# Moving the two-operand steps of attention + gated MLP from GpSimd to VectorE, under a refitted order of issue

## The chip, the core and the metric

One core of a Trainium2 chip runs the whole program in one launch. The metric is the device time of that launch in microseconds; the program ahead of the change was timed in three runs, and one more execution was profiled. TensorE (PE, with its weight loads as PEld), VectorE (DVE), ScalarE (ACT), GpSimd (POOL) and SyncE (SP, which issues every DMA) run their own streams in order, and wait for each other by semaphores.

## What is computed

Eight batches of 12-head attention over 448 positions with head size 64 and a capped score, then a gated MLP with a spatial mix:

```python
B, H, S, D = 8, 12, 448, 64                      # float32 throughout
scores = cap * tanh((q @ k.T) / sqrt(D) / cap)   # cap = 30
attn = softmax(scores)                           # denominator + 1e-9
x = concat_heads(attn @ v)                       # (8, 448, 768)
h = relu(x @ w_in)                               # w_in 768 x 1024
u, v = h[..., :512], h[..., 512:]
v_n = (v - mean(v)) / sqrt(var(v) + 1e-6)
v_s = einsum('ts,bsd->btd', w_spatial, v_n) + b_spatial[:, None]
out = (u * v_s) @ w_out                          # w_out 512 x 768
```

## The kernel before

**Work.** Heads go in pairs: 48 pairs, six to a batch. For one pair PE makes the scores (`sc`, into `ps_s`, 28 tile products of 64x224), ACT takes tanh (L553) and exp (L558) into `tp`, and PE multiplies with `v` (`pv`, L568, into `ps_x`, which has one buffer). For the first eight pairs PE also sums the exponentials with a matrix of ones (`ones`, L610, read out by ACT at L614). DVE takes maxima (and from the ninth pair on the sums) over `tp` in trees (L588, L596, L598), which go to DRAM and back (`md`, `dt`); DVE finishes them there (L632, L637) and takes the reciprocal (L639). Two more DMAs carry it to DRAM (`rd`) and broadcast it back over the partitions (`rr`, L642). ACT meanwhile copies `ps_x` to `xf` (`xev`, L573).

**The two-operand steps.** Matrix products of the MLP are made from high and low parts in a rounded format, so each operand is split. For a pair: `xmul` multiplies `xf` by `rr` (L658), `xh` copies the high part into `xg` (L309), `xl` subtracts it for the low part (L305), `xt` copies a tail (L309). In the MLP of a batch (`moe`): four chains for v (L713 to L718) are read out, normalised on DVE (L736 to L744), copied to `vh` and subtracted to `vl` (L305); four chains for u (L691 to L693); four gate chains g over `vh`, `vl` (L782 to L787), each followed by `gmul` on DVE (L792, into `o`), a copy on ACT and `gl`, the subtraction into `xg` (L305); and six output chains (L807 to L809), evicted by ACT and stored. The first batch also splits the weights, on POOL, DVE and ACT (L374 to L381).

`BND_X`, `BND_G`, `BND_VN` name the engine of each step by a letter (P POOL, V DVE, A ACT): `"PAVA"` is xmul on POOL, xh on ACT, xl on DVE, xt on ACT; `"AP"` is a copy on ACT and a subtraction on POOL.

**What sets the order.** Nothing is ordered by hand. Each step is a task with an engine, a duration, dependences, buffers and a key; a key is the pair's number plus an offset from the table `BND_KEY` (or `BND_W_KEYS` for weights). `Plan.order` (L71) plays the tasks through a model of the engines: an engine that is free takes the task with the lowest key that is ready. In the model a PE task of another kind than the last one has `STICK` added to its key, and steps with the mark `lock` (all of POOL, most of DVE) never run together. A DMA lands by the formula at L155. The result is the order of issue; the chip's engines then follow it, each stream in order, waiting where data is late.

Of the kernel before, what the change touches and what calls it, by code (L numbers as in the profile page):

```python
# [21 lines left out]
QB = 14  # L22
# [20 lines left out]
class Plan:  # L43
# [27 lines left out]
    def order(self):  # L71
        free = dict(self.cap)
        turn = {}
        for t in sorted(self.tasks, key=lambda t: (t.key, t.seq)):
            for u in t.allocs:
                turn.setdefault(u.tag, []).append(u)
        turn = {g: (l[::-1]) for g, l in turn.items()}
        live = set()

        def lacks(t):  # L80

            need = {}
# [24 lines left out]
        while done < len(self.tasks):  # L107
            if not events:
                raise RuntimeError(f"no task can start: {[(t.name, t.key) for l in avail.values() for t in l][:20]} {free}")
            now = heapq.heappop(events)  # L110
            while events and events[0] <= now:
                heapq.heappop(events)
            while fins and fins[0][0] <= now:
                _, _, t = heapq.heappop(fins)
                done += 1
                for u in t.uses:
                    left[u] -= 1
                    if not left[u]:
# [12 lines left out]
            again = True  # L131
            while again:
                again = False
                for e in engs:
                    while pend[e] and pend[e][0][0] <= now:
                        avail[e].append(heapq.heappop(pend[e])[2])
                    if busy[e] > now or not avail[e]:
                        continue
                    fit = [t for t in avail[e] if not (t.lock and ports > now) and not lacks(t)]
                    if not fit:  # L140
                        continue
                    took = min(fit, key=lambda t: (t.key + (self.STICK if t.mode != mode and e == "T" else 0.0), t.seq))
                    avail[e].remove(took)
                    for u in took.allocs:
                        free[u.tag] -= 1
                        turn[u.tag].pop()
                        live.add(u)
                    took.start, took.end = now, now + took.dur
                    if e == "T":
                        took.end += self.TURN[took.mode] if took.mode != mode else 0.0  # L150
                        mode = took.mode
                    if took.lock:
                        ports = took.end
                    if e == "S":
                        dma = max(dma, took.end + 650.0) + took.lat  # L155
                        took.lat = dma + 1000.0 - took.end
                    busy[e] = took.end
                    out.append(took)
                    heapq.heappush(fins, (took.end + took.lat, took.seq, took))
                    heapq.heappush(events, took.end + took.lat)  # L160
                    heapq.heappush(events, took.end)
                    again = True
        self.length = now
        return out

MM, MMW, TR = 203, 229, 109
FF = 760
HW, HH, XL, XF = 475, 650, 50, 4 / 360  # L170
# [12 lines left out]
def dve(n):  # L183
    return 1.04 * n + 70
# [10 lines left out]
def gpc(n):  # L195
# [26 lines left out]
CAP_BITS = 0x42200000  # L222
ANY_KEY = dict(moe=0.5, span=12.0, mv=0.0)
ANY_W_KEYS = 2.0, 0.5, 8.0, 9.0, 1.0
BND_KEY = dict(ld=-21.99, vld=-20.83, sc=-4.54, th=26.01, ex=-43.74, pv=-2.08, sm=0.15,
               mx=0.17, dn=3.16, ev=8.76, x=0.83, moe=1.42, span=10.72, step=0.16, mv=-3.27)
BND_V_FIRST = 1
WARM, WARM_N = 9, 512
BND_W_KEYS = 13.02, 0.15, 11.56, 14.75, -2.19
PE_SUMS = 8  # L230
E_W = "PAV"
W_ORDER = (0, 1)
WO_N = 256
ANY_ENG = "P", "P", "P", "VP", "AAAA", "PVPV", "AP", "VP", "V"
BND_X, BND_G, BND_VN, BND_O = "PAVA", "AP", "AP", "A"


def attn_moe(ctx, tc, bounded, shared, qk, v, qk2, v2, cap, w_in, w_sp, w_out, out):
# [408 lines left out]
    def pair(b, hp):  # L647
# [22 lines left out]
        return prev  # L670

    def moe(b, xs):
        k0 = (b + 1) * H + KEY["moe"]
        step = KEY["span"] / 18.0
        xuse, xdep = [x for x, _ in xs], [d for _, d in xs]
        us, vs, gs = [], [], []
        ks = iter([k0 + n * step for n in range(18)])

        tags = iter(["s", "s", "acc", "acc"] * 5 if bounded and b == B - 1 else ["acc"] * 18)
        kv = lambda k: k + KEY["mv"]  # L680

        def u_part(js):
            for j in js:
# [206 lines left out]
```

## Time and profile before

| | |
|---|---|
| three runs, median | 772.05 us |
| lowest, highest | 768.41, 772.09 us |
| profiled execution | 772.54 us |
| its span (first to last instruction) | 770.7 us |
| PE busy | 738.4 us, 96% |
| DVE, ACT, POOL busy | 590.6, 498.2, 213.5 us |

The span is 1.8 us shorter than the execution's time. Busy time counts an engine as busy while any of its instructions is under way. The times of TensorE's clock come as "granted clock": 1.00 is 2.4 GHz, 0.50 is 1.2 GHz, and a value between is a mean of the two over a stretch. A "wait" is idle time of an engine, put down to the instruction that ended it.

### The profile page before, as it was taken

What the parts mean: (1) busy time and instruction counts of PE and PEld (TensorE: products, weight loads), DVE (VectorE), ACT (ScalarE), POOL (GpSimd) and SP (SyncE); (2) the same over time, 40 slices, a digit from 0 to 9 for tenths busy, and PEclk for the clock granted to TensorE, in tenths of its full rate; (3) what the DMA queues carried; (4) which work ended last, traced back from release to release, by engine and by line L of the source; (5) the groups of instructions that cost most, each with busy time, mean ns of one, the idle gap of its engine ahead of it and who ended that gap; (6) DMA issues with size and microseconds to landing.
All of it is one profiled execution on the core that took longest, in us unless ns stands there. A gap on an engine that the chain in (4) does not pass through costs nothing.

```text
span 770.7 us, 19011 instructions
## 1 busy us (share of the span) xinstructions
PE 738.4 (96%) x7865; PEld 599.8 (78%) x7865; DVE 590.6 (77%) x1062; ACT 498.2 (65%) x658; POOL 213.5 (28%) x177
## 2 busy tenths in 40 slices
PE   8888898989999999999899999999999999999997
PEld 5666587777788877877688877888788877888896
DVE  4898698979998878766996788966987788976230
ACT  7988765648773684766855598357865589356221
POOL 3233225341334114221043303331033203331230
PEclk9989899999999999999999999999999999999999
DMA  7546551324320540233422334025322335013002
GB/s 260 168 159 219 163 156 49 97 94 148 123 62 16 183 136 4 78 107 132 125 62 63 123 113 134 15 85 159 126 63 74 92 113 155 25 38 100 13 1 77
DMA packets 51141, 79.23 MB, mean 103 GB/s; under 512 B 22882, under 2 KB 35684, under 8 KB 51044
## 3 DMA queue, kind: packets, MB, share of 16 engines
q1 hardware_dynamic: 51044, 77.91, 32.2%
q8 instruction: 64, 1.05, 0.5%
q14 instruction: 33, 0.27, 0.1%
HBM read 66.04 MB, written 11.81 MB: 101 GB/s over the span
## 4 chain that ended last, share of the span: by engine, by line
PE 52%; DMA 15%; DVE 15%; ACT 5%; POOL 5%; issue 4%; SPq 2%; POOLq 0%; DVEq 0%; ACTq 0%
PE ps_s L546 8%; PE ps_x L568 8%; DVE red L588 7%; DMA dt<-md 4%; DMA rr<-rd 4%; PE ps_acc L807 4%; PE ps_acc L808 3%; PE ps_acc L691 3%; PE ps_acc L809 3%; DMA md<-st 3%; PE ps_acc L692 3%; PE ps_acc L693 3%; DMA rd<-dt 3%; PE ps_acc L716 2%; PE ps_acc L718 2%
## 5 line engine op out<-in xcount | busy, mean ns | idle before, releaser
L553 ACT ACTIVATE tp<-ps_s,capt 128x896 f32<-128x896 f32 x192 | 166.5, 909 | 33.1 <-PE ps_s L546 25.2
L588 DVE TENSOR_TENSOR red<-red,tp 128x896 f32<-128x896 f32 (+1 forms) x176 | 152.7, 882 | 13.1 <-ACT tp L558 12.8
L568 PE MATMUL ps_x<-tp,v 64*64 64x224 f32 x2688 | 148.2, 362 | 11.6 <-ACT xf L573 10.4
L558 ACT ACTIVATE tp<-tp,capt 128x1792 f32<-128x1792 f32 x96 | 154.2, 1606 | 2.2
L546 PE MATMUL ps_s<-raw 64*64 64x224 f32 x2688 | 148.9, 355 | 3.4 <-ACT tp L553 3.3
L658 POOL TENSOR_TENSOR xf<-xf,rr 128x448 f32<-128x448 f32 x48 | 69.1, 1440 | 289.0 <-DMA rr<-rd 271.5
L568 PEld LDWEIGHTS ps_x<-tp,v 64*64 64x64 f32 x2688 | 105.1, 138 | 41.6 <-ACT xf L573 12.7
L546 PEld LDWEIGHTS ps_s<-raw 64*64 64x64 f32 x2688 | 99.3, 134 | 40.8 <-issue 10.7
L588 DVE TENSOR_TENSOR red<-tp 128x896 f32<-128x896 f32 x88 | 96.9, 1122 | 27.8 <-ACT tp L558 27.8
L305 POOL TENSOR_TENSOR xg<-o,xg 128x448 fp32r<-128x448 f32 x32 | 50.2, 1573 | 79.4 <-ACT xg L309 79.3
L808 PE MATMUL ps_acc<-xg,wo_h 128*128 128x448 f32 x176 | 64.8, 368 | 5.5 <-POOL xg L305 5.5
L807 PE MATMUL ps_acc<-xg,wo_h 128*128 128x448 f32 x176 | 66.7, 379 | 0.9 <-DVE o L792 0.3
L691 PE MATMUL ps_acc<-xg,wi_h 128*128 128x448 f32 x174 | 63.8, 367 | 1.8 <-DVE stg L728 1.2
L809 PE MATMUL ps_acc<-xg,wo_l 128*128 128x448 f32 x176 | 64.2, 365 | 0.0
L692 PE MATMUL ps_acc<-xg,wi_h 128*128 128x448 f32 x174 | 63.2, 363 | 0.0
L693 PE MATMUL ps_acc<-xg,wi_l 128*128 128x448 f32 x174 | 63.0, 362 | 0.0
L632 DVE TENSOR_TENSOR dt<-dt 32x28 f32<-32x28 f32 x88 | 26.1, 318 | 47.9 <-DMA dt<-md 47.8
L573 ACT COPY xf<-ps_x 128x448 f32<-128x448 f32 x48 | 46.1, 959 | 19.0 <-DVE xg L305 15.5
L309 ACT COPY o<-ps_acc 128x448 f32<-128x448 f32 x44 | 23.4, 532 | 52.5 <-PE ps_acc L809 32.8
L596 DVE STREAM_TRANSPOSE red<-red 128x448 f32<-128x448 f32 x88 | 55.1, 632 | 0.6
L588 DVE TENSOR_TENSOR red<-red 128x448 f32<-128x448 f32 x88 | 54.7, 630 | 0.1
L716 PE MATMUL ps_acc<-wi_h,xg 128*128 128x512 f32 x132 | 54.0, 409 | 0.0
(116 smaller groups left out, 1241.7 us busy)
## 6 DMA issues: line engine op xcount, KB each, us to landing
raw<-in_qk SPq DMA_DIRECT2D x48, 448.0 KB, 3.7
v<-in_v SPq DMA_DIRECT2D x48, 448.0 KB, 4.1
rr<-rd SPq DMA_DIRECT2D x96, 112.0 KB, 3.0
out<-o SPq DMA_DIRECT2D x48, 224.0 KB, 2.1
w<-in_w_in SPq DMA_DIRECT2D x12, 512.0 KB, 6.0
xg<-in_w_out SPq DMA_DIRECT2D x12, 256.0 KB, 3.0
rd<-dt SPq DMA_DIRECT2D x48, 3.5 KB, 1.5
wy<-in_w_sp SPq DMA_DIRECT2D x3, 224.0 KB, 6.3
```

Source lines behind the costliest of these rows:

```text
L546: nc.tensor.matmul(ps.t[half_rows(h), e, c % 2 * QH:(c % 2 + 1) * QH], lhsT=raw.t[half_rows(e), S + c * D:S + (c + 1) * D], rhs=raw.t[half ...
L553: lambda o=g % 2 * PW, w=w, ps=ps, tp=tp: nc.scalar.activation(out=tp.t[:, o:o + 2 * w].rearrange("p (e q) -> p e q", e=2), in_=ps.t[:, :, ...
L558: lambda tp=tp, w=w: nc.scalar.activation(out=tp.t[:, :w], in_=tp.t[:, :w], func=AF.Exp, scale=ca), [ex], [tp],
L568: nc.tensor.matmul(x.t[half_rows(e), h, :QH], lhsT=vt.t[half_rows(h), (2 * c + e) * D:(2 * c + e + 1) * D], rhs=part(c, e)[half_rows(h)], ...
L588: tt = lambda o_, i0, i1, op=op: nc.vector.tensor_tensor(o_, i0, i1, op=op)
L691: nc.tensor.matmul(ps, lhsT=wi_h[:, c, fs], rhs=x[:, XH:], start=(c == 0), stop=False)
L692: nc.tensor.matmul(ps, lhsT=wi_h[:, c, fs], rhs=x[:, :S], start=False, stop=False)
L693: nc.tensor.matmul(ps, lhsT=wi_l[:, c, fs], rhs=x[:, XH:], start=False, stop=(c == NP - 1))
L716: nc.tensor.matmul(ps, lhsT=x[:, XH:][:, ts], rhs=wi_h[:, c, FH:], start=(c == 0), stop=False)
L807: nc.tensor.matmul(ps, lhsT=wo_h[:, c, ns], rhs=g[:, XH:], start=(c == 0), stop=False)
L808: nc.tensor.matmul(ps, lhsT=wo_h[:, c, ns], rhs=g[:, :S], start=False, stop=False)
L809: nc.tensor.matmul(ps, lhsT=wo_l[:, c, ns], rhs=g[:, XH:], start=False, stop=(c == 3))
```

## The change

Three two-operand steps go from POOL to DVE in all batches: `xmul` (48), `gl` (32) and `vl` (32). On POOL stay the scaling of weights, the low part of the spatial weights and the power of the normalisation. In the model, the landing of a DMA gets 300 ns more per transfer and a shorter tail for short ones, SP's issue cost and some PE costs are changed, and `STICK` is doubled. All offsets are new, and batch 0 adds offsets of its own, `KEY0`.

```diff
-    TURN, STICK = {"N": 200.0, "K": 150.0, "R": 190.0, "C": 145.0, "Q": 130.0}, 3.87
+    TURN, STICK = {"N": 200.0, "K": 150.0, "R": 190.0, "C": 145.0, "Q": 130.0}, 8.1
...
-                        dma = max(dma, took.end + 650.0) + took.lat
-                        took.lat = dma + 1000.0 - took.end
+                        dma = max(dma, took.end + 650.0) + took.lat + 300.0
+                        took.lat = dma + (1100.0 if took.lat > 1000.0 else 500.0) - took.end
...
-MM, MMW, TR = 203, 229, 109
+MM, MMW, TR = 202, 235, 109
-HW, HH, XL, XF = 475, 650, 50, 4 / 360
+HW, HH, XL, XF = 500, 550, 50, 4 / 400
...
-BND_KEY = dict(ld=-21.99, vld=-20.83, sc=-4.54, th=26.01, ex=-43.74, pv=-2.08, sm=0.15,
+BND_KEY = dict(ld=-9.15, vld=0.69, sc=-2.3, th=36.27, ex=-132.38, pv=-0.12, sm=8.79, mx=10.7, dn=-1.77, ev=-20.83, x=-6.67, moe=11.19, span=6.93, step=0.15, mv=-18.73)
+KEY0 = dict(ld=-49.29, vld=2.7, sc=-103.24, th=-27.84, ex=31.5, pv=-29.52, sm=-1.19, mx=-50.91, dn=-18.09, ev=-50.06, x=-27.36, moe=-7.29, mv=5.22)
...
-BND_X, BND_G, BND_VN, BND_O = "PAVA", "AP", "AP", "A"
+BND_X, BND_G, BND_VN, BND_O = "VAVA", "AV", "AV", "A"
+BND_X0 = "VAVA"
+E_SEV = "A"
...
-        kk = lambda name, n=0: at + KEY[name] + KEY["step"] * n
+        kk = lambda name, n=0: at + KEY[name] + KEY["step"] * n + (KEY0.get(name, 0.0) if b == 0 else 0.0)
```

The same sum of `KEY` and `KEY0` stands in `pair` and `moe`. `E_SEV` only gives the read-out of the ones sums a name for its engine, which stays ACT. Lines from L590 on in the changed file are two or three higher than in the old one (L553 becomes L555, L658 becomes L661).

**Place 1, ACT in the first batch, around the second pair's xh.** `tp<-ps_s` is a tanh, `tp<-tp` an exp, `xg<-xf` the copies xh (448 columns) and xt (64), `xf<-ps_x` is xev of a later pair, `wi_h` a weight's high part. Before:

```order
L558 ACTIVATE tp<-tp,capt 128x1792
L553 ACTIVATE tp<-ps_s,capt 128x448
L558 ACTIVATE tp<-tp,capt 128x1344
L309 CAST xg<-xf 128x448
L614 COPY sx<-ps_acc 128x7x32
L309 CAST xg<-xf 128x64
L309 CAST wi_h<-wy 128x512
L573 COPY xf<-ps_x 128x14x32
```

And now:

```order
L555 ACTIVATE tp<-ps_s,capt 128x896
L311 CAST xg<-xf 128x448
L555 ACTIVATE tp<-ps_s,capt 128x448
L311 CAST xg<-xf 128x64
L560 ACTIVATE tp<-tp,capt 128x1344
L575 COPY xf<-ps_x 128x14x32
```

The copy xh stands earlier against the tanh and exp of the next pairs, and still ahead of a later xev.

**Place 2, the low parts of the gate in the first batch.** They stand on POOL before (`vl` ends the v part, `xf<-xf,rr` is xmul, `xg<-o` is gl, `xg<-xg` a scaling of weights):

```order
L305 TENSOR_TENSOR vl<-stg,vl 64x512
L658 TENSOR_TENSOR xf<-xf,rr 128x448
L305 TENSOR_TENSOR xg<-o,xg 128x448
L374 TENSOR_SCALAR xg<-xg 128x256
L305 TENSOR_TENSOR xg<-o,xg 128x448
```

Now they stand on DVE, where `o<-ps_acc` is gmul, `red` the trees over `tp`, `xg<-xg` the splitting of `w_out`:

```order
L795 TENSOR_TENSOR o<-ps_acc,u 128x448
L590 TENSOR_TENSOR red_163<-red_163 128x448
L590 TENSOR_TENSOR red_162<-tp 128x896
L634 TENSOR_TENSOR dt<-dt 32x2x2x7 x2
L307 TENSOR_TENSOR xg<-o,xg 128x448
L380 TENSOR_SCALAR xg<-xg 128x256
L307 TENSOR_TENSOR xg<-xf,xg 128x448
L381 SCALAR_TENSOR_TENSOR xg<-xg 128x256
L307 TENSOR_TENSOR xg<-o,xg 128x448
L795 TENSOR_TENSOR o<-ps_acc,u 128x448
```

What had a queue with little else in it stands between trees, weight splits and gmuls.

**Place 3, DVE in a later batch, from a reciprocal to the next xmul.** Before, with no xmul on DVE:

```order
L639 RECIPROCAL dt<-dt 32x28
L598 TENSOR_REDUCE st<-red_162 128x14
L305 TENSOR_TENSOR xg<-xf,xg 128x448
L598 TENSOR_REDUCE st<-red_163 128x14
L588 TENSOR_TENSOR red_162<-tp 128x896
L588 TENSOR_TENSOR red_163<-tp 128x896
```

And now, down to the xmul `xf<-xf,rr` that needs this reciprocal after its two DMAs:

```order
L641 RECIPROCAL dt<-dt 32x28
L590 TENSOR_TENSOR red_162<-red_162,tp 128x448
L739 BN_STATS lst<-stg 128x6
L598 STREAM_TRANSPOSE red_162<-red_162 128x448
L740 BN_AGGR lst<-lst 128x2
L600 TENSOR_REDUCE st<-red_162 128x14
L741 TENSOR_SCALAR lst<-lst 128x1
L600 TENSOR_REDUCE st<-red_163 128x14
L590 TENSOR_TENSOR red_162<-tp 128x896
L747 TENSOR_SCALAR stg<-stg,lst 128x512
L739 BN_STATS lst<-stg 128x6
L661 TENSOR_TENSOR xf<-xf,rr 128x448
```

Ten instructions now lie between a reciprocal and its xmul, in the same stream.

## Rows read from the trace of the kernel before

**Rows 1.** The page's first part: busy time, share of the span and instructions of each engine.

```profile
PE 738.4 (96%) x7865; PEld 599.8 (78%) x7865; DVE 590.6 (77%) x1062; ACT 498.2 (65%) x658; POOL 213.5 (28%) x177
```

**Rows 2.** Busy time by stretch: from and to, length, busy time (instructions) of each engine, granted clock, DMA share and GB/s.

```profile
0.00:96.00 96.00, 82.12 (x1441) 58.52 (x1441) 72.44 (x132) 79.22 (x101) 29.45 (x30) 0.91 0.58 193
96.00:182.00 86.00, 79.57 (x712) 65.36 (x705) 74.19 (x146) 52.21 (x75) 31.75 (x25) 0.98 0.35 107
182.00:240.00 58.00, 57.23 (x608) 45.65 (x607) 56.09 (x96) 40.52 (x53) 15.54 (x14) 1.00 0.30 91
240.00:395.00 155.00, 150.06 (x1617) 121.30 (x1616) 122.24 (x214) 104.20 (x134) 38.68 (x30) 1.00 0.33 101
395.00:450.00 55.00, 54.57 (x522) 46.67 (x521) 41.13 (x71) 31.43 (x41) 17.39 (x12) 1.00 0.27 84
450.00:765.00 315.00, 314.20 (x2979) 262.12 (x2978) 224.50 (x407) 190.05 (x256) 80.72 (x67) 1.00 0.26 81
```

**Rows 3.** PE's waits by who ended them (total us, times, longest), in 0 to 100 us, then 100 to 200 us, then 200 to 400 us (two rows).

```profile
PE ps_x L568 <- ACT xf L573: 8.3, 3, 3.7
...
PE ps_acc L808 <- POOL xg L305: 3.6, 1, 3.6
...
PE ps_acc L808 <- POOL xg L305: 1.9, 1, 1.9
PE ps_acc L718 <- DVE xg L305: 1.6, 1, 1.6
```

**Rows 4.** The stretches with granted clock 0.50 (columns as in Rows 2); the last of them, and the sum of all five, of which 16.7 us lie before 96 us.

```profile
163.30:166.60 3.30, 3.30 (x11) 2.92 (x10) 0.21 (x1) 3.26 (x4) 0.00 (x0) 0.50 0.21 74
sum 20.00, PE 18.86 PEld 13.37 DVE 13.83 ACT 17.65 POOL 6.12; mean PE 3.77 PEld 2.67 DVE 2.77 ACT 3.53 POOL 1.22
```

**Rows 5.** Groups by form: the four that are moved, the same form on DVE, and the DVE step of 512 columns; busy us, mean ns of one, idle time before and its releasers.

```profile
L658 POOL TENSOR_TENSOR xf<-xf,rr 128x448 f32<-128x448 f32 x48 | 69.1, 1440 | 289.0 <-DMA rr<-rd 271.5 <-ACT tp L553 10.0 <-DVE red L588 5.3
L305 POOL TENSOR_TENSOR xg<-o,xg 128x448 fp32r<-128x448 f32 x32 | 50.2, 1573 | 79.4 <-ACT xg L309 79.3
L305 POOL TENSOR_TENSOR vl<-stg,vh 128x512 fp32r<-128x512 f32 x24 | 32.3, 1358 | 19.9 <-ACT vh L309 19.9
L305 POOL TENSOR_TENSOR vl<-stg,vl 64x512 fp32r<-64x512 f32 x8 | 10.6, 1328 | 11.5 <-ACT vl L309 11.4
L305 DVE TENSOR_TENSOR wi_l<-wy,wi_h 128x512 fp32r<-128x512 f32 x12 | 8.3, 695 | 0.3 <-ACT wi_h L309 0.2
```

**Rows 6.** Timeline from 46.7 us: start, length, instruction, and in brackets idle time before it. The second pair's xmul, then xh, a later xev, and the `pv` that waits for it.

```profile
46.70 1.87 POOL L658 TENSOR_TENSOR xf<-xf,rr 128x448 f32<-128x448 f32 x1 [3.23 <-DMA rr<-rd]
48.60 0.56 ACT L309 CAST xg<-xf 128x448 fp32r<-128x448 f32 x1 [1.14 <-POOL xf L658]
50.06 0.94 ACT L573 COPY xf<-ps_x 128x448 f32<-128x448 f32 x1
51.05 1.40 PE L568 MATMUL ps_x<-tp,v 64*64 64x224 f32 x12 [2.81 <-ACT xf L573]
```

**Rows 7.** Timeline from 153 us: two gl on POOL, the DVE trees beside them, and the output chain that waits.

```profile
153.16 8.65 POOL L305 TENSOR_TENSOR xg<-o,xg 128x448 fp32r<-128x448 f32 x2 [4.16 <-ACT xg L309]
154.60 2.08 DVE L588 TENSOR_TENSOR red<-tp 128x896 f32<-128x896 f32 x2
156.61 2.08 DVE L588 TENSOR_TENSOR red<-red,tp 128x896 f32<-128x896 f32 x2
...
159.68 1.14 DVE L588 TENSOR_TENSOR red<-red,tp 128x448 f32<-128x448 f32 x2
161.87 0.47 PE L808 MATMUL ps_acc<-xg,wo_h 128*128 128x448 f32 x1 [3.60 <-POOL xg L305]
```

**Rows 8.** Timeline from 376.9 us: an xmul, its xh, its xl, and the v chain that waits.

```profile
376.94 1.16 POOL L658 TENSOR_TENSOR xf<-xf,rr 128x448 f32<-128x448 f32 x1 [13.45 <-DMA rr<-rd]
378.14 0.71 ACT L309 CAST xg<-xf 128x448 fp32r<-128x448 f32 x2 [0.34 <-POOL xf L658]
380.59 0.60 DVE L305 TENSOR_TENSOR xg<-xf,xg 128x448 fp32r<-128x448 f32 x1
381.24 0.50 PE L718 MATMUL ps_acc<-wi_h,xg 128*128 128x512 f32 x1 [1.60 <-DVE xg L305]
```

**Rows 9.** Timeline: two reciprocals (at 28 us and at 546 us) and the xmul that each releases through `rd` and `rr`; a DVE step on `dt` of the same form as the mean in Rows 10.

```profile
28.18 0.32 DVE L639 RECIPROCAL dt<-dt 32x28 f32<-32x28 f32 x1
34.19 1.13 POOL L658 TENSOR_TENSOR xf<-xf,rr 128x448 f32<-128x448 f32 x1 [6.70 <-DMA rr<-rd]
...
545.98 0.30 DVE L639 RECIPROCAL dt<-dt 32x28 f32<-32x28 f32 x1
553.39 0.13 DVE L632 TENSOR_TENSOR dt<-dt 32x28 f32<-32x28 f32 x1
554.35 1.16 POOL L658 TENSOR_TENSOR xf<-xf,rr 128x448 f32<-128x448 f32 x1 [22.49 <-DMA rr<-rd]
```

**Rows 10.** DVE groups by form that share two SBUF operands with POOL's steps, and DVE's longest wait after 400 us.

```profile
L632 DVE TENSOR_TENSOR dt<-dt 32x28 f32<-32x28 f32 x88 | 26.1, 318 | 47.9 <-DMA dt<-md 47.8
L588 DVE TENSOR_TENSOR red<-tp 128x896 f32<-128x896 f32 x88 | 96.9, 1122 | 27.8 <-ACT tp L558 27.8
L588 DVE TENSOR_TENSOR red<-red,tp 128x448 f32<-128x448 f32 x88 | 58.2, 668 | 0.1
...
DVE dt L632 <- DMA dt<-md: 36.1, 9, 5.3
```

More of the change, by code (lines that the diff above doesn't have):

```diff
@@ L50 @@
     SAME = {"T": 0.0, "A": 60.0, "V": 60.0, "P": 60.0, "S": 0.0}
-    TURN, STICK = {"N": 200.0, "K": 150.0, "R": 190.0, "C": 145.0, "Q": 130.0}, 3.87
-    OWN = {"vtr", "red3", "max", "mred2", "sred2", "stat", "gmul", "vadd", "xadd", "rec", "ones", "evl", "evh", "nb"}
+    TURN, STICK = {"N": 200.0, "K": 150.0, "R": 190.0, "C": 145.0, "Q": 130.0}, 8.1
+    OWN = {"vtr", "red3", "max", "mred2", "sred2", "stat", "gmul", "vadd", "xadd", "rec", "ones", "evl", "evh", "nb", "sev"}
     def __init__(self, bufs):
@@ L224 @@
 ANY_W_KEYS = 2.0, 0.5, 8.0, 9.0, 1.0
-BND_KEY = dict(ld=-21.99, vld=-20.83, sc=-4.54, th=26.01, ex=-43.74, pv=-2.08, sm=0.15,
-               mx=0.17, dn=3.16, ev=8.76, x=0.83, moe=1.42, span=10.72, step=0.16, mv=-3.27)
+BND_KEY = dict(ld=-9.15, vld=0.69, sc=-2.3, th=36.27, ex=-132.38, pv=-0.12, sm=8.79, mx=10.7, dn=-1.77, ev=-20.83, x=-6.67, moe=11.19, span=6.93, step=0.15, mv=-18.73)
+KEY0 = dict(ld=-49.29, vld=2.7, sc=-103.24, th=-27.84, ex=31.5, pv=-29.52, sm=-1.19, mx=-50.91, dn=-18.09, ev=-50.06, x=-27.36, moe=-7.29, mv=5.22)
 BND_V_FIRST = 1
 WARM, WARM_N = 9, 512
-BND_W_KEYS = 13.02, 0.15, 11.56, 14.75, -2.19
+BND_W_KEYS = -3.23, 2.34, -35.92, 5.87, -12.54
 PE_SUMS = 8
@@ L319, in st2 @@
         return {"V": dve, "P": gp}[e](n)
-    E_HI, E_Q, E_K, E_V, E_PH, E_X, E_G, E_VN, E_O = ANY_ENG
+    E_HI, E_Q, E_K, E_V, E_PH, _, E_G, E_VN, E_O = ANY_ENG
     if bounded:
-        E_X, E_G, E_VN, E_O = BND_X, BND_G, BND_VN, BND_O
+        E_G, E_VN, E_O = BND_G, BND_VN, BND_O
     def split_f32(key, c):
@@ L613, in sev @@
             def sev(h):
-                nc.scalar.copy(out=sx.t.rearrange("p (i h b) -> p h b i", h=2, b=QB // 2)[:, h],
-                               in_=acc[h].t[:, 0, :QH].rearrange("p (b i) -> p b i", i=32))
+                copy(E_SEV, sx.t.rearrange("p (i h b) -> p h b i", h=2, b=QB // 2)[:, h],
+                     acc[h].t[:, 0, :QH].rearrange("p (b i) -> p b i", i=32))
             sums = add("T", NC * QQ, kk("pv", 1) + 0.01, ones, exps, [u, w, *acc], acc, name="ones", mode="K")
-            sums = [add("A", act(QH) + 210, kk("ev"), lambda h=h: sev(h), [sums], [acc[h], sx], [sx] if h == 0 else [], name="sev")
+            sums = [add(E_SEV, act(QH) + 210 if E_SEV == "A" else dve(QH), kk("ev"), lambda h=h: sev(h), [sums], [acc[h], sx], [sx] if h == 0 else [], name="sev")
                     for h in range(2)]
@@ L655, in pair @@
             deps = [d for e in range(2) for d in head_any(b, 2 * hp + e, vt, vdep, xf, rr, after)]
+        E_X = BND_X0 if bounded and b == 0 else (BND_X if bounded else ANY_ENG[5])
         g = Buf("xg")
-        k += KEY["x"] if bounded else 1.3
+        k += KEY["x"] + (KEY0["x"] if b == 0 else 0.0) if bounded else 1.3
         m = add(E_X[0], st2(E_X[0], 448), k, lambda: eng[E_X[0]].tensor_tensor(xf.t, xf.t, rr.t, op=ALU.mult), deps, [xf, rr], name="xmul")
@@ L672, in moe @@
     def moe(b, xs):
-        k0 = (b + 1) * H + KEY["moe"]
+        k0 = (b + 1) * H + KEY["moe"] + (KEY0["moe"] if bounded and b == 0 else 0.0)
         step = KEY["span"] / 18.0
@@ L679, in moe @@
         tags = iter(["s", "s", "acc", "acc"] * 5 if bounded and b == B - 1 else ["acc"] * 18)
-        kv = lambda k: k + KEY["mv"]
+        kv = lambda k: k + KEY["mv"] + (KEY0["mv"] if bounded and b == 0 else 0.0)
         def u_part(js):
```

## Prediction

> **What bounds the kernel now.** I read the busy times first. PE is busy for 96% of the span, DVE for 77%, ACT for 65%, POOL for 28% [rows 1]. A busy PE bounds a kernel only where it has work at hand all the time, so the next view is the same by stretch [rows 2]. PE idles 13.9 us before 96 us, 6.4 us from 96 to 182, 0.8 us to 240, 4.9 us to 395, and 1.2 us in the 370 us from there to 765. From 395 us on PE is the bound and nothing that other engines do faster can be seen in the time. What can be won lies ahead of it: the first batch, which runs softmax pairs on ACT and DVE and splits the weights meanwhile, and a few waits up to 395 us. The third view, TensorE's clock, adds to this. It was at 1.2 GHz for 20.0 us in all, 16.7 us of it before 96 us and 3.3 us at 163 us [rows 4], each time behind a wait of PE. PE's 18.9 us of work there would have taken half at 2.4 GHz, so these stretches cost about 9.4 us: 1.65 us at 163 us, 7.8 us before.
>
> The fourth view says whom PE waited for [rows 3]. In the first 100 us it is xev, 8.3 us in three waits. At one of them the timeline shows the chain [rows 6]: the xmul on POOL takes 1.87 us, xh stands behind it on ACT, xev stands behind xh in ACT's stream, and `pv` cannot have the one `ps_x` buffer before xev. At 158 us it is a gl on POOL, 3.6 us; two gl took 8.65 us together while DVE ran its trees [rows 7]. At 336 us it is a gl again, 1.9 us, and at 380 us an xl on DVE, 1.6 us [rows 3, 8].
>
> **Part 1: what the moved steps cost on DVE.** POOL loses 48 + 32 + 24 + 8 steps of 69.1 + 50.2 + 32.3 + 10.6 = 162.2 us [rows 5]. On DVE two trees of 448 columns take 1.14 us, so 0.57 us each back to back [rows 7]; a subtraction of 512 columns has a mean of 0.695 us, of which I count 0.65 [rows 5]. The 80 steps of 448 columns then take 45.6 us, the 32 of 512 take 20.8 us: DVE gets 66 us. Some comes back, because DVE's two-operand steps now stretch when POOL runs one. The `dt` step has a mean of 318 ns and is seen at 0.13 us [rows 9, 10]; 88 of them give 16 us. `red<-tp` has 1122 ns against 1.04 us (2.08 for two), 88 times 0.08 is 7 us; the trees with `tp` of 448 columns have 668 ns against 0.57, 88 times 0.1 is 9 us [rows 7, 10]. That is 32 us from three groups. DVE would end at 590.6 + 66 - 32 = 625 us, or 81%: still under PE's 96%, so on the average it doesn't become the bound.
>
> **Part 2: the gl of the first batch (place 2).** The wait of 3.6 us and the slow clock behind it, 1.65 us, hang on POOL's turn between DVE's trees [rows 3, 4, 7]. On DVE nobody competes with gl, but it stands in a stream with trees, weight splits and gmuls, and DVE is busy for 74.2 of 86 us there [rows 2]. The bounds are -5.3 us (the wait goes) and 0 (gl comes as late). I take -3.3, since two trees of 1.04 us ahead of it is what the new order shows at worst.
>
> **Part 3: the waits from 240 to 395 us.** POOL's gl at 336 us: -1.9 us, by the same reason. At 380 us the chain is xmul 1.16, xh, and an xl that starts 1.7 us after xh's end [rows 8]; only xmul gets shorter, by 0.6 us. Together -2.5 us, with bounds of -4.9 (all idle time of the stretch, [rows 2]) and +1.
>
> **Part 4: the first batch up to 96 us (place 1).** The three waits for xev and the slow clock make 8.3 + 7.8 = 16.1 us. The new order does not cut the chain: xh still stands ahead of a later xev, and still waits for the landing of `rr`. What certainly changes is the xmul, 1.87 us on POOL against 0.57 [rows 6, 7], 1.3 us in each of three waits: -3.9 us. The bounds are far apart: -16 us if the offsets of batch 0 set xh behind the landings for good, and +4 us if xmul, now in DVE's stream, holds trees and weight splits until `rr` has landed. I take -4, the value that a row supports.
>
> **Part 5: steady batches.** Behind an xmul that waits for `rr` now stand DVE's trees, `dt` steps and subtractions, and behind those ACT's exp buffers and PE's next chains. From a reciprocal to its xmul the chip took 5.7 us at 28 us (28.50 to 34.19) and 8.1 us at 546 us (546.28 to 554.35) [rows 9]. At place 3 the ten instructions between them are two trees (0.57 and 1.04 us), and by estimate from the rows of trees some 3.4 us for the other eight: about 5 us. So each xmul may hold DVE for 0.7 to 3.1 us, 1.9 in the middle. DVE idles 315.0 - 224.5 = 90.5 us from 450 to 765 us [rows 2], some 25 us in each 88 us batch (8 batches in the span, the last ones alike). The moved steps take 10 x 0.57 + 4 x 0.65 = 8.3 us of that, six waits of 1.9 us take 11.4 us: 19.7 of 25 us. The cover holds, the cost is 0; if it goes, see the second rival. PE's own work stays: the order has as many turns between tile kinds per batch as before, twelve.
>
> **The sum.** Profiled execution 772.5 us, less 3.3, less 2.5, less 4.0: **762.7 us**. That execution stands 0.5 us above the median of the three runs, 772.05 us, so the same sum holds for a median.
>
> **Rival 1: DVE takes PE's place from 96 to 240 us, and the gain is lost there.** DVE is busy for 130.3 of these 144 us now, 56.1 of the last 58 [rows 2]. The moved steps of that stretch (nine xmul, eight gl, eight vl by the order) take 17 x 0.57 + 8 x 0.65 = 15 us; if half comes back from stretching, DVE needs 138 of 144 us, and can't be early for anything. Then parts 2 and 4 fall to nothing and part 3 stays: 770.0 us. For it speaks how full DVE is, against it that DVE's trees in this very stretch are stretched by POOL. The Trainium skill, "Perfetto Trace Analysis", section "Optimizing Scalar/DVE Operations", argues on this side: work may go from a saturated VectorE to GpSimd, and since the two share a read port, shifting it between them might not help. The trace agrees on the sharing (8.65 us for two gl, [rows 7]) and shows DVE saturated only in these 58 us.
>
> **Rival 2, slower: xmul holds DVE's stream.** If landings come 3.1 us behind xmul's place on the mean, as at 546 us, six waits take 18.6 us and the moved steps 8.3 us, 26.9 of 25 us: DVE falls back 1.9 us in each of seven batches, 13 us, and parts 2 and 4 are gone as well: 772.5 + 13 - 2.5 = 783 us. It decides from 2.8 us per xmul. For it: the two latencies shown, and DVE's wait for `md`, 36.1 us in nine pieces after 400 us [rows 10], the same kind of wait. Against it: trees wait for exps anyway, so much of this time is idle already.
>
> **Rival 3: batch 0 is freed.** If all of parts 2 to 4 comes at its lower bound: 772.5 - 5.3 - 4.9 - 16.1 = 746 us. For it speaks that batch 0 gets offsets of its own and that each avoided wait saves its slow clock too; against it that xh and xev keep their places.
>
> That the change does nothing is no rival: the order shows the steps on DVE and the streams rearranged.
>
> **How the numbers follow.** The forecast (756 to 768 us) gets 0.52, rival 1 0.22, rival 3 0.14, rival 2 0.12. The range is 749 to 775 us: it takes in the forecast and rival 1 with the upper bounds of parts 2 to 4, most of rival 3, and leaves out rival 2 and the far end of rival 3, together under 0.2. About 0.5% is what a measurement of this kernel can tell from no change; that is 768.2 to 775.9 us. Forecast and rival 3 lie below: faster 0.66. Rival 1 lies within: 0.22. Rival 2 lies above: 0.12.
>
> **What would show it right or wrong.** Part 1: POOL's busy time falls by some 160 us, DVE's comes to 615 to 635 us, and the `dt` mean falls to under 0.2 us. Part 2: no wait of an output chain for gl, no slow clock near 163 us. Part 3: PE idle from 240 to 395 us of 2 to 3 us. Part 4: PE's waits for xev shrink, and the first MLP product starts 3 to 5 us ahead of 96 us. Part 5: DVE waits at xmul for `rr`, 60 to 100 us in all, with PE's idle time after 395 us unchanged. Wrong would be a PE that waits for DVE's gl, vl or xl in every batch (rival 2), or only from 96 to 240 us (rival 1), or a PE that never falls to 1.2 GHz in the first 96 us (rival 3).

## The result

The changed kernel takes 752.56 us (median of four runs, 750.37 to 753.20), the one before 772.07 us in the same session (four runs, 768.41 to 774.54). The ratio is 0.9746, with a 95% interval of 0.9702 to 0.9790: faster by 19.5 us, where 9.4 us were forecast. The profiled execution of after took 750.37 us, with a span of 748.6 us, 22.1 us less than the 770.7 us of before.

**Engines.** The page's first part, after, beside [rows 1]:

```profile
PE 729.3 (97%) x7865; PEld 598.3 (80%) x7865; DVE 616.5 (82%) x1174; ACT 495.7 (66%) x658; POOL 62.4 (8%) x65
```

DVE has 112 instructions more and only 25.9 us more busy time. PE, with the same products, is busy for 9.1 us less; some 4.3 of that is its clock, next (half of 18.9 less 10.2 us of work at 1.2 GHz).

**Stretches.** The windows of [rows 2] over after, then its stretches at half clock, beside [rows 4] (columns as there):

```profile
0.00:96.00 96.00, 85.16 (x1486) 63.75 (x1487) 79.17 (x149) 83.91 (x109) 29.83 (x25) 0.95 0.65 205
96.00:182.00 86.00, 84.18 (x861) 67.28 (x863) 81.44 (x166) 57.73 (x79) 8.88 (x12) 1.00 0.37 113
182.00:240.00 58.00, 57.82 (x601) 48.04 (x597) 56.60 (x109) 40.18 (x53) 3.55 (x4) 1.00 0.28 83
240.00:395.00 155.00, 154.20 (x1613) 126.47 (x1604) 132.39 (x252) 104.28 (x135) 7.28 (x8) 1.00 0.33 103
...
11.20:14.60 3.40, 3.40 (x44) 2.44 (x40) 3.30 (x3) 3.27 (x3) 2.98 (x3) 0.51 1.00 371
62.40:65.80 3.40, 3.40 (x40) 2.26 (x44) 3.40 (x10) 3.40 (x7) 0.00 (x0) 0.51 0.57 139
76.00:79.40 3.40, 3.40 (x44) 2.35 (x39) 2.86 (x5) 2.55 (x4) 1.59 (x2) 0.50 0.53 190
```

Up to 395 us PE idles 13.6 us, against 26.0 before. It is at 1.2 GHz for 10.2 us instead of 20.0, and not once from 80 us to its last product.

**PE's waits** of after, from 0 to 100 us (two rows) and from 100 to 200 us, beside [rows 3]:

```profile
PE ps_s L548 <- ACT tp L555: 6.1, 4, 3.3
PE ps_x L570 <- ACT xf L575: 3.4, 2, 2.0
...
PE ps_s L548 <- ACT tp L555: 1.7, 3, 1.1
```

No gl and no xl is left among them; xev has 3.4 us of 8.3.

**DVE's groups** of after by form, beside [rows 5, 10]: the moved steps, then three groups that shared with POOL before. The last two rows are DVE's waits for DMAs over the whole span.

```profile
L661 DVE TENSOR_TENSOR xf<-xf,rr 128x448 f32<-128x448 f32 x48 | 30.2, 629 | 17.8 <-DMA rr<-rd 17.4 <-ACT xf L575 0.2
L307 DVE TENSOR_TENSOR xg<-o,xg 128x448 fp32r<-128x448 f32 x32 | 19.5, 609 | 2.6 <-ACT xg L311 2.6
L307 DVE TENSOR_TENSOR vl<-stg,vh 128x512 fp32r<-128x512 f32 x24 | 16.1, 679 | 0.2
L307 DVE TENSOR_TENSOR vl<-stg,vl 64x512 fp32r<-64x512 f32 x8 | 5.5, 689 | 0.5 <-ACT vl L311 0.3
L634 DVE TENSOR_TENSOR dt<-dt 32x28 f32<-32x28 f32 x88 | 14.2, 168 | 14.7 <-DMA dt<-md 14.6
L590 DVE TENSOR_TENSOR red<-tp 128x896 f32<-128x896 f32 x88 | 93.1, 1076 | 22.6 <-ACT tp L560 22.6
L590 DVE TENSOR_TENSOR red<-red,tp 128x448 f32<-128x448 f32 x88 | 53.4, 612 | 0.5
...
DVE xf L661 <- DMA rr<-rd: 17.4, 16, 6.8
DVE dt L634 <- DMA dt<-md: 14.6, 15, 3.2
```

The moved steps take 71.3 us on DVE, and its other steps give back 45.4 us (590.6 + 71.3 - 616.5).

**Where the time went.** Windows at fixed times don't hold the same work in two kernels, so I count PE's lost time by place in the program: the start of a product less the work that PE was given before it, with 203 ns for a product of 128x448, 232 ns for 128x512, 47.3 ns for 64x224 and 90 ns for each turn between those of 64x224 and the others, as they follow each other in the trace where PE waits for nothing. The work is 710.6 us before and 710.8 us after. Up to four of the five places both kernels give PE the same work to within 1 us; up to the end of batch 0's MLP after gives it 133 us and before 143, because the new order puts fewer later pairs ahead of that place. Lost time holds idle time, slow clock, and waits too short to show as idle. Each column is the loss in a stretch of the program, in us, from one profiled execution:

| kernel | up to the first MLP product | to the end of batch 0's MLP | to the end of batch 1's gate | to the end of batch 3's v | to the end | sum |
|---|---|---|---|---|---|---|
| before | 28.2 | 9.8 | 2.3 | 8.3 | 6.1 | 54.7 |
| after | 21.4 | 1.9 | 2.8 | 3.0 | 2.8 | 31.9 |
| gain | 6.8 | 7.9 | -0.5 | 5.3 | 3.3 | 22.8 |

The gain is spread over four of the five stretches, the last one included, where I had expected none. The two profiled executions lie 22.2 us apart and the medians 19.5, so some 3 us of the 22.8 belong to these two executions.

### The profile page after: what moved, and what is told of

Read it like the earlier page. It is cut to its first block, busy times and chain, and to the rows that moved or that the text cites. A ratio compares the mean times of both kernels' runs of the same rounds, so it can differ in the third digit from the quotient of the medians.

```text
span 748.6 us, 18868 instructions
## 1 busy us (share of the span) xinstructions
PE 729.3 (97%) x7865; PEld 598.3 (80%) x7865; DVE 616.5 (82%) x1174; ACT 495.7 (66%) x658; POOL 62.4 (8%) x65
## 4 chain that ended last, share of the span: by engine, by line
PE 67%; DVE 15%; DMA 11%; ACT 2%; issue 2%; POOL 1%; SPq 1%; DVEq 0%; ACTq 0%
PE ps_s L548 11%; PE ps_x L570 11%; DVE red L590 5%; PE ps_acc L810 4%; PE ps_acc L812 4%; PE ps_acc L811 4%; PE ps_acc L694 4%; PE ps_acc L695 4%; PE ps_acc L696 4%; PE ps_acc L719 3%; PE ps_acc L721 3%; PE ps_acc L720 3%; DMA rd<-dt 3%; DMA rr<-rd 3%; PE ps_acc L788 2%
## 5 line engine op out<-in xcount | busy, mean ns | idle before, releaser
L555 ACT ACTIVATE tp<-ps_s,capt 128x896 f32<-128x896 f32 x192 | 168.0, 911 | 20.6 <-PE ps_s L548 15.6
L548 PE MATMUL ps_s<-raw 64*64 64x224 f32 x2688 | 150.8, 355 | 8.3 <-ACT tp L555 8.1
L590 DVE TENSOR_TENSOR red<-red,tp 128x448 f32<-128x448 f32 (+1 forms) x176 | 148.0, 853 | 10.1 <-ACT tp L560 9.2
L570 PE MATMUL ps_x<-tp,v 64*64 64x224 f32 x2688 | 145.5, 355 | 3.9 <-ACT xf L575 3.9
L548 PEld LDWEIGHTS ps_s<-raw 64*64 64x64 f32 x2688 | 98.1, 133 | 46.7 <-ACT tp L555 16.2
L570 PEld LDWEIGHTS ps_x<-tp,v 64*64 64x64 f32 x2688 | 103.6, 135 | 32.7 <-ACT xf L575 6.0
L590 DVE TENSOR_TENSOR red<-tp 128x896 f32<-128x896 f32 x88 | 93.1, 1076 | 22.6 <-ACT tp L560 22.6
L743 POOL TENSOR_TENSOR lst<-lst,capt 128x1 f32<-128x1 f32 x32 | 27.4, 857 | 561.3 <-DVE lst L741 547.1
L810 PE MATMUL ps_acc<-xg,wo_h 128*128 128x448 f32 x176 | 64.6, 367 | 0.1
L811 PE MATMUL ps_acc<-xg,wo_h 128*128 128x448 f32 x176 | 63.6, 361 | 0.0
L719 PE MATMUL ps_acc<-wi_h,xg 128*128 128x512 f32 x132 | 54.7, 414 | 0.0
L590 DVE TENSOR_TENSOR red<-red 128x448 f32<-128x448 f32 x88 | 53.7, 618 | 0.5
L600 DVE TENSOR_REDUCE st<-red 128x14 f32<-128x448 f32 x88 | 51.5, 610 | 1.0
L720 PE MATMUL ps_acc<-wi_l,xg 128*128 128x512 f32 x132 | 52.2, 395 | 0.0
```

The lines of the kernel that those rows point to most:

```text
L548: nc.tensor.matmul(ps.t[half_rows(h), e, c % 2 * QH:(c % 2 + 1) * QH], lhsT=raw.t[half_rows(e), S + c * D:S + (c + 1) * D], rhs=raw.t[half ...
L555: lambda o=g % 2 * PW, w=w, ps=ps, tp=tp: nc.scalar.activation(out=tp.t[:, o:o + 2 * w].rearrange("p (e q) -> p e q", e=2), in_=ps.t[:, :, ...
L570: nc.tensor.matmul(x.t[half_rows(e), h, :QH], lhsT=vt.t[half_rows(h), (2 * c + e) * D:(2 * c + e + 1) * D], rhs=part(c, e)[half_rows(h)], ...
L590: tt = lambda o_, i0, i1, op=op: nc.vector.tensor_tensor(o_, i0, i1, op=op)
L719: nc.tensor.matmul(ps, lhsT=x[:, XH:][:, ts], rhs=wi_h[:, c, FH:], start=(c == 0), stop=False)
L810: nc.tensor.matmul(ps, lhsT=wo_h[:, c, ns], rhs=g[:, XH:], start=(c == 0), stop=False)
```

## The experiments

My theory after the result: the engine and the order of issue need each other. On POOL the steps come late and stretch DVE's; on DVE they cost little only if the order puts xmul where `rr` has landed. Rivals: the move alone gives the gain; the order alone does. Where an order is "kept", the plan is made with the old letters or the new, and only the issuing engine differs, so that PE, ACT and SP have the same rows. Ratios are to the kernel before, timed on the same chip in the same session (medians there 770.55, 769.82 and 770.56 us), with 95% intervals; losses by stretch are as in the table above, from one profiled execution each. The work is between 709.3 and 710.8 us in all of them but e13 (718.1).

| run | order | xmul | gl, vl | us | ratio | losses by stretch |
|---|---|---|---|---|---|---|
| e1 | before's | DVE | DVE | 768.48 | 0.998 (0.995 to 1.001) | 27.3, 5.3, 1.4, 2.9, 10.0 |
| e14 | before's | POOL | DVE | 761.43 | 0.988 (0.985 to 0.992) | 25.2, 5.5, 1.7, 5.4, 6.2 |
| e2 | after's | POOL | POOL | 764.11 | 0.991 (0.988 to 0.995) | 25.7, 3.2, 5.0, 6.6, 3.7 |
| e7 | after's | POOL | DVE | 757.64 | 0.983 (0.980 to 0.985) | 26.4, 2.7, 3.0, 4.0, 4.1 |
| e16 | after's | DVE | POOL | 755.84 | 0.982 (0.978 to 0.985) | 24.3, 2.7, 2.5, 8.4, 2.9 |
| e5 | after's | batch 0 POOL | batch 0 POOL | 758.81 | 0.986 (0.982 to 0.989) | 26.3, 2.5, 2.3, 4.5, 3.6 |
| e6 | after's | batch 0 DVE | batch 0 DVE | 758.75 | 0.986 (0.982 to 0.990) | 21.0, 2.6, 3.9, 5.3, 4.7 |
| e3 | old tables, new letters | DVE | DVE | 758.97 | 0.985 (0.980 to 0.991) | 25.5, 4.4, 0.6, 4.8, 5.9 |
| e4 | no `KEY0` | DVE | DVE | 774.96 | 1.006 (1.003 to 1.009) | 44.2, 7.6, 0.7, 2.2, 3.8 |
| e11 | after's offsets in batch 0 only | DVE | DVE | 813.10 | 1.055 (1.051 to 1.059) | 23.2, 32.1, 8.9, 14.6, 18.5 |
| e10 | new model, old offsets | DVE | DVE | 786.32 | 1.020 (1.017 to 1.022) | 23.5, 7.9, 1.2, 11.9, 28.8 |
| e13 | old model, new offsets | DVE | DVE | 764.65 | 0.992 (0.989 to 0.994) | 25.8, 1.8, 3.3, 4.3, 6.3 |

**e1, the move alone.** The kernel before, planned with its own letters; the three lambdas issue on VectorE:

```diff
-lambda: eng[E_X[0]].tensor_tensor(xf.t, xf.t, rr.t, op=ALU.mult)
+lambda: eng["V"].tensor_tensor(xf.t, xf.t, rr.t, op=ALU.mult)
...
-sub(e1, vl.t, v2(), f(vh.t))
+sub("V", vl.t, v2(), f(vh.t))
...
-sub(e1, g.t[:, :S], gt.t, f(g.t[:, XH:]))
+sub("V", g.t[:, :S], gt.t, f(g.t[:, XH:]))
```

> The order of before is kept for PE, ACT and SP, row for row; only the 112 steps xmul, gl and vl go to VectorE, at the places in the order that they had. The engine theory (the move itself gives the gain: no stretched DVE steps, no late POOL steps) expects about 760 us, DVE steps unstretched, PE's waits for gl gone and its half-clock time down from 20 us towards 10. The order theory (the refitted order gives the gain) expects 768 to 776 us: an xmul that was planned for POOL now holds DVE until rr has landed.

768.48 us, no measurable difference, at the edge of what the order theory expected. Part 2 and part 3 happen (5.3 and 2.9 us lost, against 9.8 and 8.3), but 3.9 us more are lost in the last stretch. PE's waits there, after 395 us, and DVE's for `rr`:

```profile
PE ps_acc L718 <- DVE xg L305: 3.8, 3, 1.7
PE ps_acc L807 <- DVE o L792: 1.8, 3, 0.7
...
DVE xf L658 <- DMA rr<-rd: 17.8, 12, 5.0
```

One of them in the timeline (start, length, instruction, idle time before it):

```profile
455.04 0.62 DVE L658 TENSOR_TENSOR xf<-xf,rr 128x448 f32<-128x448 f32 x1 [1.56 <-DMA rr<-rd]
455.59 0.64 DVE L596 STREAM_TRANSPOSE red<-red 128x448 f32<-128x448 f32 x1
455.90 0.70 ACT L309 CAST xg<-xf 128x448 fp32r<-128x448 f32 x2
...
457.51 1.07 DVE L588 TENSOR_TENSOR red<-tp 128x896 f32<-128x896 f32 x1
458.51 0.60 DVE L305 TENSOR_TENSOR xg<-xf,xg 128x448 fp32r<-128x448 f32 x1
459.17 0.50 PE L718 MATMUL ps_acc<-wi_h,xg 128*128 128x512 f32 x1 [1.15 <-DVE xg L305]
```

The xmul holds DVE for 1.56 us, all that stands behind it is late by as much, the xl at 458.51 too, and PE waits 1.15 us: rival 2's chain. The profiled execution of e1 (764.85 us) is near the lowest of its twelve (763.99 to 773.23 us), so the losses in the table show less than the median does.

**e14, xmul back on POOL in the old order.** The edit is e1's without its first pair of lines.

> The order of before, kept on PE, ACT and SP; gl and vl on VectorE, xmul back on POOL. In the run with all three on VectorE PE waited 3.8 us for xl and 1.8 us for gmul after 395 us, and DVE waited 33.5 us for rr at xmul. Theory one, xmul planned for POOL holds DVE's stream: without it these waits of PE are gone, PE loses 6 us or less after 395 us instead of 10, and the run is 3 to 6 us faster than with all three moved. Theory two, DVE is simply fuller by gl and vl: the waits for xl stay and the time is that of all three moved.

761.43 us: theory one, and a little beyond the 3 to 6 us that it expected. 0.010 of the time, 7 us, is what xmul on DVE costs in the old order. The losses in the last stretch show 3.8 us of it (10.0 against 6.2); where the rest lies isn't shown. After 395 us the waits for xl are gone; what PE waits for there is this:

```profile
PE ps_acc L807 <- DVE o L792: 1.2, 4, 0.6
PE ps_acc L716 <- ACT xg L309: 0.9, 1, 0.9
```

**e2, the order alone.** The kernel after, with `"P"` in the three lambdas of e1.

> The order of after is kept for PE, ACT and SP; the 112 steps are issued on POOL instead of VectorE, at the places that the order gives them. The order theory expects 753 to 758 us, PE's idle time nearly that of after. The engine theory expects 766 to 772 us, with DVE stretched by about 40 us in all as before and PE waiting for gl, vl or xl again.

764.11 us, between the two theories. The order alone gives 0.9%, the move alone 0.2% (at the interval's end 0.5), both together 2.5%: by these medians more than half exists only with both. DVE's `dt` step is stretched again:

```profile
L634 DVE TENSOR_TENSOR dt<-dt 32x28 f32<-32x28 f32 x88 | 24.4, 284 | 16.4 <-DMA dt<-md 16.4
```

**e7 and e16, one group of steps each in the new order.** e7 is after with `"P"` for xmul, e16 with `"P"` for gl and vl.

> The order of after, kept on PE, ACT and SP; xmul back on POOL, gl and vl on VectorE. Theory one, the refitted order gives xmul a place in DVE's stream at which rr has landed: then xmul on DVE is a gain here, where it was a loss of 7 us in the old order, and this kernel takes 756 to 760 us. Theory two, xmul on DVE costs its waits in any order: this kernel takes 746 to 751 us, faster than after.

> The order of after; gl and vl back on POOL, xmul on VectorE. If the two groups of steps add up, this run and the one with xmul alone on POOL lose together what all 112 on POOL lose, about 12 us; then 756 to 760 us here. If the lock is what costs, either group on POOL brings most of the loss back: 759 to 763 us in both.

757.64 us: theory one. The same move of xmul that costs 7 us in the old order gains some 6 us in the new (0.9825 to 0.9746). DVE's waits for `rr` agree with the theory's reason. This is after's row from 395 us on, to be compared with that of e1:

```profile
DVE xf L661 <- DMA rr<-rd: 10.4, 8, 6.8
```

In each run one long wait (6.8 us in after, 5.0 in e1) belongs to the last batch. Without it DVE waits 3.6 us in seven pieces in after and 12.8 us in eleven in e1, and PE waits for no xl in after.

e16 takes 755.84 us, just under the range of the additive answer: the two groups are worth 0.008 and 0.007 of the time, 0.015 together, and all 112 steps 0.017 (e2). The place where e7 loses most, from its timeline, and then the same place of after:

```profile
72.12 1.13 POOL L661 TENSOR_TENSOR xf<-xf,rr 128x448 f32<-128x448 f32 x1 [0.63 <-DMA rr<-rd]
73.28 0.56 ACT L311 CAST xg<-xf 128x448 fp32r<-128x448 f32 x1 [0.25 <-POOL xf L661]
75.45 1.69 POOL L661 TENSOR_TENSOR xf<-xf,rr 128x448 f32<-128x448 f32 x1 [2.20 <-DMA rr<-rd]
77.17 0.86 ACT L311 CAST xg<-xf 128x448 fp32r<-128x448 f32 x3 [3.33 <-POOL xf L661]
78.67 0.99 ACT L555 ACTIVATE tp<-ps_s,capt 128x896 f32<-128x896 f32 x1
79.71 1.77 PE L548 MATMUL ps_s<-raw 64*64 64x224 f32 x16 [7.04 <-ACT tp L555]
```

```profile
72.19 0.63 DVE L661 TENSOR_TENSOR xf<-xf,rr 128x448 f32<-128x448 f32 x1 [0.90 <-DMA rr<-rd]
72.89 0.86 ACT L311 CAST xg<-xf 128x448 fp32r<-128x448 f32 x3 [0.48 <-issue]
74.39 0.99 ACT L555 ACTIVATE tp<-ps_s,capt 128x896 f32<-128x896 f32 x1
75.43 1.29 PE L548 MATMUL ps_s<-raw 64*64 64x224 f32 x16 [3.28 <-ACT tp L555]
```

The xh stands in ACT's stream ahead of a tanh, and PE's scores wait for that tanh: 7.04 us with xmul on POOL, 3.28 with it on DVE. Of these 3.8 us the longer xmul is 1.1 us (1.69 against 0.63). The rest is `rr`, which lands later in e7: its xmul starts at 75.45 us against 72.19, and PE is only 0.5 us behind. Why it lands later isn't shown. In e16, with xmul on DVE, PE waits longer than in after at the same place, too:

```profile
77.53 1.77 PE L548 MATMUL ps_s<-raw 64*64 64x224 f32 x16 [5.42 <-ACT tp L555]
```

Up to the first MLP product three runs of this order have the same xmul on POOL (e2, e5, e7: 25.7, 26.3, 26.4 us lost) and three on DVE (after, e6, e16: 21.4, 21.0, 24.3). The means differ by 3.9 us and the groups don't overlap, but executions of what is the same program up to there differ by up to 3 us, so a single cell of the table isn't to be read closer.

**e5 and e6, batch 0 or the rest.** e5 is after with `"P" if b == 0 else "V"` in the three lambdas, e6 with the letters exchanged.

> The order of after, kept on PE, ACT and SP; the moved steps of batch 0 alone (6 xmul, 4 gl, 4 vl) are issued on POOL, those of the other batches on VectorE. With all 112 on POOL, PE lost 4.3 us more than after up to the first MLP product and 1.3 us more up to the end of the first output chains. If that is batch 0's own steps, 757 to 759 us, with the stretch after 240 us as in after. If the loss came from POOL's long queue as a whole, 752 to 755 us.

> The order of after; batch 0's moved steps on VectorE, those of the other seven batches on POOL. If the lock's stretching (36 us of DVE time after 100 us in the run with all steps on POOL) and late POOL steps cost steady time too, 757 to 760 us, the loss lying between 160 and 395 us. If batches 1 to 7 are bound by PE whatever the engine, 752 to 754 us.

Both as the first theory of each had it, 6 us above after by the medians and 8 to 9 us by the ratios (0.011). The two halves together (0.0225) are more than all 112 steps (0.017), so they don't add up as xmul and the low parts do; the intervals, some 0.004 either way, leave room for that. In e5 the loss is ahead of the first MLP product (26.3 us against 21.4), in e6 behind it (2.6 + 3.9 + 5.3 + 4.7 = 16.5 against 10.5), a third of it in the last stretch, where its theory had none.

**e3, the old tables with the new letters.** One line of the kernel before:

```diff
-BND_X, BND_G, BND_VN, BND_O = "PAVA", "AP", "AP", "A"
+BND_X, BND_G, BND_VN, BND_O = "VAVA", "AV", "AV", "A"
```

> The kernel before with the three engine letters changed and nothing else: the order is planned anew with the old offsets, the old landing model and no offsets for batch 0. The engine theory expects 755 to 762 us. The order theory expects about 768 to 775 us: the old model lands a DMA too early, so xmul stands too early in DVE's stream.

758.97 us, the engine theory's number but not its reason: against e1 the only difference is that the planner knows where the steps run, and that gives 1.3%. PE's waits for xl after 395 us are down to one of 0.4 us, and DVE's for `rr` there to 7.2 us in seven pieces beside that of the last batch (4.9 us). So of the whole 2.5% the letters with a plan made for them give 1.5, and the refitted tables 1.1 more.

**e4, e11, e10, e13, pieces of the tables.** e4 sets all of `KEY0` to 0.0; e10 is e3 with after's model (`STICK`, landing, costs); e13 is after with the old model; e11 gives the common table of before to batches 1 to 7, all but the offset of the v loads:

```diff
-        kk = lambda name, n=0: at + KEY[name] + KEY["step"] * n + (KEY0.get(name, 0.0) if b == 0 else 0.0)
+        KB = KEY_B0 if b == 0 else KEY
+        kk = lambda name, n=0: at + KB[name] + KB["step"] * n
```

> The kernel after with batch 0's own offsets all zero, so that batch 0 is planned by the common table. If batch 0's offsets carry the gain up to the first output chain, 760 to 768 us, with PE losing 33 us or more by the end of the first MLP instead of 23, and the stretch after 240 us as in after. If the move and the common table carry it, 751 to 756 us.

> After's model and letters, and batch 0 with after's offsets, weights too; the offsets of batches 1 to 7 are those of before except the place of the v loads, since with that one too no order exists. If batch 0's offsets carry what the new order wins, 752 to 757 us, PE losing 24 us or less by the end of the first output chains. If the steady offsets carry it, 758 to 763 us, as in the run with the old tables planned anew.

> The kernel before with the new engine letters and the new model (landing, costs, STICK), but the old offsets and none for batch 0. If the model of landings is what lets xmul stand on DVE, 752 to 757 us, and DVE waits less than 20 us for rr at xmul. If the offsets are, 758 to 770 us, no better than the old model with the same letters (759 us).

> The kernel after with the old model (landing, costs, STICK 3.87) under the new offsets. If the offsets carry the order's gain, 752 to 757 us. If they only fit the model that they were found with, 760 to 780 us, the loss lying in batch 0.

e4, 774.96 us: without its own offsets batch 0 loses 44.2 us up to the first MLP product. That is no worth of `KEY0` over the old table, which lost 28.2: the new common table doesn't suit batch 0. e4, e10 and e11 are slower than every forecast made for them, and slower than before by 0.6, 2.0 and 5.5%. e13 is still 0.8% faster than before. Its loss against after isn't in batch 0 alone, as its theory had it: under the old model PE turns 165 times between the pairs' products and the others instead of 83 times, 7.3 us of work that the losses leave out. Every piece without the others is slower than all of the new tables together (after) and slower than none of them (e3), so how much the landing model gives and how much the offsets stays open. None of the twelve is faster than after.

## Why the prediction was off by half

The direction was right, and so were the mechanisms of parts 1 to 3 as far as they went; four terms of the sum were too small. Forecast 9.8 us (3.3 + 2.5 + 4.0 + 0), measured 22.8 in lost time, 19.5 by the medians. That 752.56 us lies inside the stated range is luck: it is in the part of the range that was opened for rival 3, below the forecast's 756 to 768 us.

- **Part 1, DVE's load: right, and mis-sized both ways.** DVE 616.5 us against 625 and within 615 to 635; `dt` at 168 ns, under the 0.2 us promised. The moved steps cost 71.3 us, not 66. The three groups gave back 11.9 + 3.8 + 4.8 = 20.5 us, not 32, but other steps that I had not counted gave 25 more.
- **Part 4, the first batch: -4.0 forecast, -6.8 measured.** The first MLP product starts at 90.1 us instead of 96.2, where 3 to 5 us were promised. The size of the term agrees with the move (3.9 us between the three runs with xmul on POOL and the three with it on DVE), but not its reason. I had taken 1.3 us off each of three waits for xev. Between these two groups the mean of PE's waits for xev up to 95 us falls only from 3.5 to 2.7 us; that of its waits for tanh falls from 9.4 to 7.0 us, and at the largest of those most is the landing of `rr` (e7). So the agreement is luck. The rest, 2 to 3 us, is the order with the steps still on POOL (28.2 to 25.7 in e2). I had given the order nothing, because "xh still stands ahead of a later xev": I argued only from what it leaves in place.
- **Part 2, 96 to 182 us: -3.3 forecast, -7.9 measured.** The wait for gl and the slow clock at 163 us went, as said: even the move in the old order gives 4.5 us (e1). But the same stretch had 6.4 us of idle time [rows 2], and I priced only the 3.6 us of it that hang on gl. The order takes nearly all of it, on whatever engine gl runs: 3.2 us are left with all steps on POOL (e2), 2.5 with batch 0's alone there (e5), 1.9 in after.
- **Part 3, 240 to 395 us: -2.5 forecast, -5.3 measured.** That is beyond my bound of -4.9, which was the stretch's idle time alone. PE's idle time fell from 4.9 to 0.8 us; the remaining 1.2 us came out of what counted as busy. The move does this in either order (8.3 to 2.9 in e1; 6.6 to 3.0 from e2 to after), and more by gl and vl than by xmul (4.0 with those on DVE in e7, 8.4 with xmul alone there in e16).
- **Part 5, steady batches: 0 forecast, -3.3 measured.** Two errors of opposite sign. DVE waits 17.4 us for `rr` at xmul, not 60 to 100: I had put each xmul about 5 us behind its reciprocal, as at place 3, and given all six of a batch the middle of two latencies. In after 32 of the 48 xmuls find `rr` landed. And I said that nothing that other engines do faster can be seen after 395 us. In before, each batch starts its output chains right behind the gate, and PE waits for gmul to free the accumulator, in pieces that hardly show as idle. From the timeline of before:

```profile
424.52 0.47 PE L807 MATMUL ps_acc<-xg,wo_h 128*128 128x448 f32 x1 [0.31 <-DVE o L792]
...
425.46 0.60 DVE L792 TENSOR_TENSOR o<-ps_acc,u 128x448 f32<-128x448 f32 x1
425.63 0.37 PE L809 MATMUL ps_acc<-xg,wo_l 128*128 128x448 f32 x1
426.12 0.47 PE L807 MATMUL ps_acc<-xg,wo_h 128*128 128x448 f32 x1
```

  The last two start 0.49 us apart instead of 0.20, and the second starts as the gmul above it ends (426.06). In after, 5.7 us of score and `pv` products stand between gate and output chains (404.7 to 410.4 us), and the wait is gone. By start times the output chains of this stretch lose 3.4 us before and 0.4 in after. With the steps still on POOL the order gives the stretch 2.4 us (e2): most of this gain is the order's.
- **Rival 2** had the true mechanism of the slower side, and the order decides whether it comes: e1 pays 3.9 us in the last stretch for it, after nothing. **Rival 1** did not come: DVE is busy for 138.0 of the 144 us from 96 to 240 us, as it had said, but PE waits for tanh for 1.7 us there, and for DVE for 0.2 us. The Trainium skill's advice in "Perfetto Trace Analysis", section "Optimizing Scalar/DVE Operations", that shifting work between VectorE and GpSimd might not help, agrees with e1 (0.2%). It doesn't agree with e14, where the order is the same and gl and vl alone on VectorE gain 1.2%.
- **Rival 3** (746 us) gave a time nearer to the result than the forecast's, for another reason: batch 0 was not freed of its waits and slow clock (21.4 us still lost), and later stretches made up for it.

The step that failed is the making of the sum: each term was the wait that the trace names at a moved step, and the order got no term of its own. Alone it is worth 6.4 us by the medians (770.55 to 764.11 in e2; 10.5 us of lost time between the two single executions), and it is what turns xmul on DVE from a loss of 7 us into a gain of 6. A sum of terms for the moved steps holds neither. Which of the new offsets does this stays open (e4, e10, e11, e13).

## What to carry to other kernels

When steps move to an engine whose stream has other work, judge the move only together with a plan that knows it: the same xmul cost 7 us in an order made for the other engine and gained 6 in one made for this. Where a change also rewrites the order, bound its worth by all of the bounding engine's loss in each stretch (start times less the work given to it), not by the waits that the profile names. Tables that were fitted together are tested together: pieces of them came out between 0.8% faster and 5.5% slower than the kernel before.

## What the runs showed of the hardware that I had not expected

The sharing between POOL and DVE reaches a DVE step with only one operand of 512 columns. The normalisation (`stg`, with one scalar per partition from `lst`) fell from a mean of 665 to 540 ns:

```profile
L747 DVE TENSOR_SCALAR stg<-stg,lst 128x512 f32<-128x512 f32 x32 | 17.3, 540 | 3.4 <-POOL lst L743 3.2
```

In the eight kernels that have none of batch 1 to 7's moved steps on POOL (after, e1, e3, e4, e5, e10, e11, e13) its mean is 534 to 543 ns; in the six that have some there (before, e2, e6, e7, e14, e16) it is 562 to 665 ns.

POOL's scaling of weights of 512 columns went the other way, from a mean of 1124 ns to 1843 ns:

```profile
L376 POOL TENSOR_SCALAR wy<-w 128x512 f32<-128x512 f32 x12 | 22.1, 1843 | 46.4 <-DMA w<-in_w_in 32.7 <-DVE ws_l L307 7.0 <-DVE wi_l L307 6.1
```

That is 8.6 us of the 11 by which POOL's busy time fell less (151 us) than the moved steps had taken (162 us). It isn't shown to come from the fuller DVE: the same twelve steps have means of 986 ns in e3 and 989 in e10, with all 112 steps on DVE, and 1345 in e6, whose first batch is the program of after.
